# Second mixture of an attention + two-mixture kernel: results kept in PSUM until their split, preparation issued by elapsed products, a second combining buffer, copies of partial sums issued first

## The chip, the cores and the metric

The kernel runs on one core of a Trainium2 chip. The metric is the device time of one execution in microseconds (us), median over runs. TensorE (PE) multiplies, VectorE (DVE), ScalarE (ACT) and GpSimd (POOL) do the elementwise work, SyncE (SP) issues the DMAs. Each engine works through its own list of instructions in order, and semaphores tie the lists together.

## The reference

Clustered attention (queries see only keys of their own cluster), then two feed-forward "mixtures". The change lies in the second:

```python
def _moe2_ref(x, w_gate, w_val, w_out):      # x 1536 x 512, d_ff = 1536
    g = x @ w_gate
    silu = g * (1.0 / (1.0 + np.exp(-g)))
    val = x @ w_val
    return (silu * val @ w_out).astype(np.float32)
```

## The kernel before

Attention fills the first part of the execution, the first mixture the time up to about 517 us, the second mixture the rest. All products are made of fp32r halves: an operand is split into a rounded high part (ACT copies it, "hi") and the remainder (DVE or POOL subtract, "lo"), and a product takes three matmuls (high*high, high*low, low*high).

The weights come in as doubles, in blocks of 128 x 512. A block is loaded into one of two `raw` buffers (line 78), its bits are put together to fp32 by ACT (`block_shift`, line 82) and DVE (lines 91 and 95) in a buffer `cw`, and then split.

**Sets.** The second mixture has 12 blocks f of 128 hidden columns, taken in pairs, and two halves u of the tokens (2 x 384 each): 24 sets `(f, u)` in the order (2k,0) (2k+1,0) (2k,1) (2k+1,1). Weights of f are used by two sets, two places apart. Sets 0 to 3 are plain (`run_plain`): for each e of the two token quarters a gate product g and a value product v (12 matmuls each, a bank of PSUM each), then `v_plain` (ACT sigmoid, DVE sigmoid*g) and `v_plain2` (DVE times v, ACT hi, DVE lo). Sets 4 to 23 use Winograd's form of Strassen's scheme (`run_set`): seven products P1, P2, P6, P7, P5, P3, P4 of 6 matmuls (x 384 columns) instead of eight, in three banks A, B and C (`BANK`, line 946). Bank A runs on: P1 is summed into it, a copy p1 of the partial sum is taken by ACT (`snap`, line 971), P6 is added, copy u2, P5 is added, copy u4, P3 is added. So P6 can't start before copy p1 is done, P5 not before u2, P3 not before u4. The gates and values are then put together by DVE and ACT:

- `v_ga`: p1 + B is the gate of quarter 0; `v_sa`: its sigmoid (ACT); `v_gs`: their product.
- `v_vb`: u4 + C; `v_sb`: sigmoid of A (the gate of quarter 1); `v_b`: A*sigmoid, times u4.
- `v_a`: u2 + C, times the gate product. `hi2`/`lo2` split the two results into g.

Between the products stand six `piece`s per set: 3 matmuls x 512 columns each, which multiply the g of earlier sets by w_out into four banks of their own (`ps_a`); after each second f their sums are moved on (`evac2`, lines 1032 to 1042: DVE adds, or ACT copies and POOL adds). A, B, C of a set, and g0, v0, g1, v1 of a plain set, come from a ring of four banks, `ps_h`: a product waits until the bank's last reader of four allocations ago is done.

**Preparation.** The scheme needs sums of the weights S1 to S4 (POOL, `w_sum`, line 785) and, per half u, sums of the inputs T1 to T4 (DVE, `y_sum`, line 767), each split as well (hi: lines 799 and 759; lo: lines 803 and 763). These steps are `tasks` with an engine and a list of steps that must have been issued before. `hook(engine, n)` (line 1054) stands at fixed places of the sets and issues the first n tasks of that engine whose needs were issued; `finish` forces tasks that a set is about to use. Whether a task's data is there yet doesn't count in the choice.

Of the kernel before, what the change touches and what calls it, by code (L numbers as in the profile page):

```python
# [20 lines left out]
def tile_kernel(ctx, tc, q_t, k_t, q_s, k_s, v_l, cent, w_in, w_out, a_co, b_co, w_gate, w_val, w_o2, out):  # L21
# [4 lines left out]
    P = 128  # L26
# [589 lines left out]
    with ExitStack() as mctx:  # L616
# [126 lines left out]
        cq = cw[:, 0:4 * DM].rearrange("p (i n) -> p i n", i=8)  # L743
# [41 lines left out]
        def w_sum(q):  # L785
# [12 lines left out]
        def w_hi(f, to, frm):  # L798
            nc.scalar.copy(out=w_of(f)[:, 0, to], in_=cq[:, frm])

        def w_lo(f, to, frm):
            w = w_of(f)
# [6 lines left out]
        def c_of(n):  # L809
            key, f, _ = loads[n]  # L810
            i = n % 5 if n < N1 else {"v": 0, "g": 1, "p": 4}[key]
            return cw[:, i * DM:(i + 1) * DM]
# [134 lines left out]
        live2 = {}  # L947

        def short(name):
            return ring(tmp, "short", 10, C3)  # L950

        def pe(s, p):
# [6 lines left out]
            n, last = 0, 6 * (len(terms) // 2) - 1  # L959
            for a, b in zip(terms[::2], terms[1::2]):  # L960
# [20 lines left out]

        def v_ga(s):
            dve(s, "p1", "p1", "B", ALU.add)

        def v_sa(s):
            sigmoid(s, "sa", "p1")

        def v_gs(s):
            dve(s, "p1", "p1", "sa", ALU.mult)
# [7 lines left out]
        def v_b(s):  # L997
            dve(s, "sb", "A", "sb", ALU.mult)
            dve(s, "u4", "u4", "sb", ALU.mult)

        def v_a(s):
            dve(s, "u2", "u2", "C", ALU.add)
            dve(s, "u2", "u2", "p1", ALU.mult)

        def hi2(s, e):
            f, u = sets[s]
            g = g_hl[2 * u + e, f] = g_tile(6, C3)
            nc.scalar.copy(out=g[:, 0, :], in_=live2[s, "u4" if e else "u2"])

        def lo2(s, e):  # L1010
            f, u = sets[s]
            g = g_hl[2 * u + e, f]
            nc.vector.tensor_tensor(  # L1013
                out=g[:, 1, :], in0=live2[s, "u4" if e else "u2"], in1=r32(g[:, 0, :]), op=ALU.subtract
            )
# [3 lines left out]
        def piece(f, j, c, bank=None):  # L1019
# [3 lines left out]
            g, w = g_hl[j, f], wt_of["p", f]  # L1023
            for m, (wi, gi) in enumerate(((0, 0), (1, 0), (0, 1))):
# [7 lines left out]
        def evac2(f, j, c, on_dve):  # L1032
# [5 lines left out]
            else:  # L1038
                ts = tmp[:, 10 * C3:10 * C3 + T]
# [8 lines left out]
        done = set()  # L1048
        asked = set()

        def task(name, engine, needs, fn):
            tasks[name] = (engine, needs, fn)

        def hook(engine, n=1):
            for name in list(tasks):
                eng, needs, fn = tasks[name]
                if n and eng == engine and done.issuperset(needs):
                    del tasks[name]
                    fn()
                    done.add(name)  # L1060
                    n -= 1

        def finish(names):
            for name in names:
                if name in tasks:
                    eng, needs, fn = tasks.pop(name)
                    finish(needs)
                    fn()
                    done.add(name)

        def begin(n):
            while len(started) < min(n, len(loads)):
                block_start()

        def to_prepare(f):
# [15 lines left out]
            for q, needs in ((S1, [(f, "v", "bits")]), (S3, [(f, "v", "bits"), (f, "g", "bits")]), (S2, [(f, S1), (f, S3)]),  # L1091
                             (S4, [(f, S2)])):
                task((f, q), "pool", needs, lambda q=q: w_sum(q))
            A, Sq = slice(0, 3), slice(3, 7)
            task((f, "hi a"), "act", [(f, "g", "bits")], lambda: w_hi(f, A, slice(1, 4)))
# [4 lines left out]
            task((f, "hi p"), "act", [(f, "p", "bits")], lambda: block_hi(started[b + 2], p_place(f)))  # L1100
# [18 lines left out]
        done.update((0, q, "lo") for q in (B11, B12, B21, B22))  # L1119

        def v_plain(s, e):

            name = "u4" if e else "u2"
            live2[s, name] = short(name)
            nc.scalar.activation(out=live2[s, name], in_=live2[s, f"g{e}"], func=AF.Sigmoid)
            dve(s, name, name, f"g{e}", ALU.mult)

        def v_plain2(s, e):
            name = "u4" if e else "u2"
            dve(s, name, name, f"v{e}", ALU.mult)  # L1130
            hi2(s, e)
            lo2(s, e)

# [8 lines left out]
        to_combine(0, [], (T4, T2))  # L1142
        pe(0, "g0")
        hook("dve", 2)
# [4 lines left out]
        hook("dve", 2)  # L1149
        pe(0, "v0")  # L1150
        v_plain2(0, 0)
        mm, ev = project(*seq[NS - 1])
        for fn in mm:
            fn()
        for e in ev:
            e()
        to_combine(1, [B11, B21, B12, B22], (B21, B22, T4, T2))
        hook("act", 2)
        pe(0, "g1")
        hook("dve")  # L1160
        v_plain(0, 1)
        hook("dve")
        hook("pool")
        pe(0, "v1")
        hook("act", 2)
        v_plain2(0, 1)
        hook("dve", 2)
        hook("pool")
# [9 lines left out]
        def run_plain(s, fill):  # L1178
            fill = list(fill)
            n = (len(fill) + 2) // 3  # L1180
            for e in range(2):
                pe(s, f"g{e}")
                hook("act")
                hook("dve")
                hook("pool")
                v_plain(s, e)
                hook("act")
                hook("dve")
                some(fill, n)
                pe(s, f"v{e}")  # L1190
                hook("act")
                hook("dve")
                hook("pool")
                some(fill, len(fill) if e else n // 2)
                v_plain2(s, e)
                hook("dve")

        def run_set(s, fill):
            fill = list(fill)
            f, u = sets[s]  # L1200
# [5 lines left out]
            hook("dve")  # L1206
            pe(s, "P2")
            hook("act")
# [111 lines left out]
```

## Time and profile before

| | |
|---|---|
| three runs, median (range) | 839.53 us (835.87 to 840.25) |
| profiled execution: time / span | 839.48 / 837.7 us |
| busy PE / DVE / ACT / POOL | 94% / 76% / 61% / 56% |
| granted clock, mean | 0.986 |
| second mixture, sets 4 to 23 | 564.80 to 824.43 us |

PE is busy 94% of the span, so the question in any stretch is what PE waits for there and at which clock it runs. Between 300 and 507 us PE has no gap. In the second mixture it has many short ones, each ended by the copy of a partial sum, and a few ended by POOL or DVE. Other engines' idle time only matters where it ends such a gap.

### The profile page before, as it was taken

Reading aid. Unit: us, or ns where it says so; the run is one execution under the profiler, and the core shown is the slowest. Engines: PE = TensorE matmul, PEld = TensorE weight load, DVE = VectorE, ACT = ScalarE, POOL = GpSimd, SP = SyncE. Lnnn points to the kernel's source line nnn. Section 1 sums busy time; section 2 is a strip of 40 time slices with the busy share of each in tenths; the row PEclk is TensorE's granted clock in tenths of the full one; section 3 lists DMA queues with packets and bytes.
Section 4 is the critical chain, followed back from the end, with each engine's and each line's share of the span. In section 5 each row is a group of like instructions: output and inputs, shape, how many; then the busy total and the mean of one; then the engine's idle time right before and its main releaser. Section 6 shows DMA issues by size and latency. Waiting matters only on the chain.

```text
span 837.7 us, 11534 instructions
## 1 busy us (share of the span) xinstructions
PE 791.4 (94%) x4080; PEld 638.0 (76%) x4080; DVE 635.3 (76%) x923; ACT 512.0 (61%) x982; POOL 466.9 (56%) x379
## 2 busy tenths in 40 slices
PE   5999999999999999999999999888997999899997
PEld 4666666666658788888888888877886888888896
DVE  6877788778669999889888898844686766756654
ACT  5767676777776878787687775444534454444431
POOL 3656687557335776767776967643354554444511
PEclk8999999999999999999999999988999999999999
DMA  5256435542222212121112010021211112121013
GB/s 172 92 192 201 146 103 174 194 139 68 70 95 75 76 51 76 50 67 42 69 51 76 27 50 26 1 75 56 97 51 56 70 51 76 50 76 51 1 38 113
DMA packets 26553, 67.94 MB, mean 81 GB/s; under 512 B 4448, under 2 KB 9536, under 8 KB 26496
## 3 DMA queue, kind: packets, MB, share of 16 engines
q1 hardware_dynamic: 26496, 67.21, 24.2%
q8 instruction: 32, 0.52, 0.3%
q14 instruction: 25, 0.20, 0.1%
HBM read 59.48 MB, written 3.19 MB: 75 GB/s over the span
## 4 chain that ended last, share of the span: by engine, by line
PE 57%; DVE 19%; ACT 9%; issue 6%; DMA 5%; POOL 4%; ACTq 0%; DVEq 0%; SPq 0%; POOLq 0%
PE h_ps L664 11%; PE acc L720 10%; PE c_ps L965 9%; PE acc L1025 7%; PE o_ps L437 7%; PE t_ps L426 5%; DVE tmp L976 5%; PE s_ps L368 4%; DMA raw<-w_o_dram 3%; PE s_ps L372 3%; DVE g L1013 2%; DVE st L380 2%; DVE part L1037 1%; DMA raw<-w_out_dram 1%; POOL tmp L681 1%
## 5 line engine op out<-in xcount | busy, mean ns | idle before, releaser
L965 PE MATMUL c_ps<-r,wb 128*128 128x384 f32 x648 | 128.7, 340 | 13.4 <-ACT tmp L973 9.8
L965 PEld LDWEIGHTS c_ps<-r,wb 128*128 128x128 f32 x648 | 115.1, 189 | 23.6 <-ACT tmp L973 13.8
L380 DVE TENSOR_REDUCE st<-s_ps 128x1 f32<-128x768 f32 x96 | 91.4, 952 | 31.7 <-PE s_ps L372 31.2
L388 ACT ACTIVATE p<-s_ps,st 128x768 f32<-128x768 f32 x96 | 87.6, 913 | 19.9 <-DVE st L380 18.3
L431 ACT COPY pt<-t_ps 128x384 f32<-128x384 f32 x160 | 70.2, 485 | 36.1 <-PE t_ps L426 36.0
L681 POOL TENSOR_TENSOR tmp<-tmp 128x512 f32<-128x512 f32 x46 | 65.8, 1431 | 46.1 <-ACT tmp L680 45.7
L82 ACT ACTIVATE raw<-raw 128x512 f32<-128x512 f32 x68 | 45.8, 675 | 60.4 <-DMA raw<-w_o_dram 33.8
L426 PE MATMUL t_ps<-ident,p 128*128 128x128 f32 x576 | 79.8, 274 | 1.0 <-ACT pt L431 0.8
L965 PE MATMUL c_ps<-r,xw 128*128 128x384 f32 x336 | 68.2, 345 | 10.4 <-ACT tmp L973 8.3
L976 DVE TENSOR_TENSOR tmp<-tmp,c_ps 128x384 f32<-128x384 f32 x76 | 41.6, 547 | 44.5 <-ACT tmp L973 39.5
L791 POOL TENSOR_TENSOR cw<-cw 128x256 f32<-128x256 f32 x40 | 33.1, 832 | 75.3 <-DVE cw L95 74.6
L965 PEld LDWEIGHTS c_ps<-r,xw 128*128 128x128 f32 x336 | 60.8, 192 | 16.2 <-ACT tmp L973 10.4
L704 POOL TENSOR_TENSOR g<-td,tmp 128x512 fp32r<-128x512 f32 x46 | 61.0, 1326 | 20.9 <-DVE td L699 20.9
L437 PE MATMUL o_ps<-pt,v 128*64 128x384 f32 x384 | 72.3, 498 | 0.0
L426 PEld LDWEIGHTS t_ps<-ident,p 128*128 128x128 f32 x576 | 67.3, 141 | 6.3 <-ACT p L388 1.1
L720 PE MATMUL acc<-g,r 128*128 128x512 f32 x288 | 71.1, 396 | 0.3 <-ACT part L727 0.3
L1025 PE MATMUL acc<-wb,g 128*128 128x512 f32 x216 | 62.3, 410 | 2.6 <-ACT part L1035 2.6
L720 PEld LDWEIGHTS acc<-g,r 128*128 128x128 f32 x288 | 53.9, 188 | 13.8 <-ACT part L727 0.8
L664 PE MATMUL h_ps<-r 128*128 128x512 f32 x252 | 61.5, 393 | 0.0
L368 PE MATMUL s_ps<-k,q 128*128 128x512 f32 x192 | 58.7, 387 | 2.4 <-ACT p L388 2.2
L1041 POOL TENSOR_TENSOR part<-tmp,part 128x512 f32<-128x512 f32 x19 | 24.7, 1299 | 60.3 <-ACT tmp L1040 60.3
L664 PEld LDWEIGHTS h_ps<-r 128*128 128x128 f32 x252 | 47.1, 188 | 12.3 <-issue 1.8
(155 smaller groups left out, 1788.5 us busy)
## 6 DMA issues: line engine op xcount, KB each, us to landing
raw<-w_in_dram SPq DMA_DIRECT2D x16, 512.0 KB
raw<-w_out_dram SPq DMA_DIRECT2D x16, 512.0 KB
raw<-w_val_dram SPq DMA_DIRECT2D x12, 512.0 KB
raw<-w_gate_dram SPq DMA_DIRECT2D x12, 512.0 KB
raw<-w_o_dram SPq DMA_DIRECT2D x12, 512.0 KB
xa<-q_t_dram SPq DMA_DIRECT2D x14, 384.0 KB
xa<-k_t_dram SPq DMA_DIRECT2D x14, 384.0 KB
sq<-q_s_dram SPq DMA_DIRECT2D x8, 384.0 KB
```

The source lines that it names most:

```text
L368: nc.tensor.matmul(s_ps[:, lo:hi], t["q1"][:, qs], t["k1"][:, lo:hi], start=True, stop=False)
L380: nc.vector.tensor_reduce(out=st[:, 0, k:k + 1], in_=live["s", b, hp, half, i, e], axis=AX.X, op=ALU.max, negate=True)
L388: nc.scalar.activation(out=p, in_=live.pop(("s", b, hp, half, i, e)), func=AF.Exp, bias=st[:, 0, k:k + 1], accum_out=st[:, 1, k:k + 1],)
L426: nc.tensor.transpose(t_ps[:, j, :], p[:, kb * P:(kb + 1) * P], ident)
L431: nc.scalar.copy(out=pt[:, ks, qc], in_=t_ps)
L437: nc.tensor.matmul(live["o", b, hp, half][e * D:(e + 1) * D, :], heads[b, 2 * hp + e]["v"][:, kb, :], live["pt", b, hp, half, e][:, kb, :] ...
L664: nc.tensor.matmul(h_ps, w[:, wi, cs], x[:, xi, cc, :], start=(n == 0), stop=(n == 3 * NCC - 1))
L681: spread.tensor_tensor(out=tq, in0=tq, in1=tr, op=ALU.add)
L720: nc.tensor.matmul(acc[c], w[:, wi, cs], g[:, gi, :], start=(first and m == 0), stop=(last and m == 2))
L965: nc.tensor.matmul(live2[key], set_of[f][:, wi, a, cs], x[xi][:, kc, :], start=(first and n == 0), stop=(n == last), skip_group_check=True,)
L976: eng.tensor_tensor(out=live2[s, out], in0=live2[s, a], in1=live2[s, b], op=op)
L1025: nc.tensor.matmul(acc2[j, c], g[:, gi, c * P:(c + 1) * P], w[:, wi, :], start=(f % 2 == 0 and m == 0), stop=(f % 2 == 1 and m == 2),)
```

## The change

PE and the DMAs keep their order; the lists of ACT, DVE and POOL are reordered.

- Sums and products are written back to their PSUM bank: `v_ga` and `v_gs` write to B, `v_b` to A, `v_a`'s product to B, the plain sets' product to v's bank, and hi2/lo2 read them there. Bank C comes from `ps_a` instead of `ps_h`.
- In `run_set` a snap stands directly behind its product, ahead of piece, sigmoid and hook.
- Odd f above 1 gather their weights in a second buffer `cqs[1]` in `tmp`, so only f-2's splits must be done before f's bits, not f-1's. The ring of short buffers shrinks from 10 to 5 for that.
- `clk` counts products issued (1 for 6 matmuls of 384 columns, 0.65 for a piece). A task is taken only if each need comes from its own engine or was issued at least LAG units ago (ACT, DVE 1.7; POOL 3.5; DMA 5.5). Splits also wait for the set from which their place is free.
- Hooks stand at more places, also ahead of set 1, and weights of f = 2 and 3 are asked for earlier.

```diff
-        cq = cw[:, 0:4 * DM].rearrange("p (i n) -> p i n", i=8)
+        cqs = [
+            t.rearrange("p (i n) -> p i n", i=8) for t in (cw[:, 0:4 * DM], tmp[:, 5 * C3 + T:5 * C3 + T + 4 * DM])
+        ]
...
         def short(name):
-            return ring(tmp, "short", 10, C3)
+            return ring(tmp, "short", 5, C3)
...
-                live2[key] = ps_h.tile([P, T], F32, tag="h", name="c_ps")[:, 0:C3]
+                bank = ps_a.tile([P, T], F32, tag="acc", name="c_ps") if key[1] == "C" else ps_h.tile(
+                    [P, T], F32, tag="h", name="c_ps")
+                live2[key] = bank[:, 0:C3]
...
         def v_ga(s):
-            dve(s, "p1", "p1", "B", ALU.add)
+            dve(s, "B", "p1", "B", ALU.add)
...
         def v_gs(s):
-            dve(s, "p1", "p1", "sa", ALU.mult)
+            dve(s, "B", "sa", "B", ALU.mult)
...
         def v_b(s):
-            dve(s, "sb", "A", "sb", ALU.mult)
-            dve(s, "u4", "u4", "sb", ALU.mult)
+            dve(s, "A", "sb", "A", ALU.mult)
+            dve(s, "A", "u4", "A", ALU.mult)
...
         def v_a(s):
             dve(s, "u2", "u2", "C", ALU.add)
-            dve(s, "u2", "u2", "p1", ALU.mult)
+            dve(s, "B", "u2", "B", ALU.mult)
...
+        LAG = {"act": 1.7, "dve": 1.7, "pool": 3.5, "dma": 5.5, "set": 0.0}
+        def in_time(eng, by, at):
+            return by == eng or at + LAG[by] <= clk[0]
...
-                if n and eng == engine and done.issuperset(needs):
+                if n and eng == engine and all(x in done and in_time(eng, *done[x]) for x in needs):
...
-                before = [x for x in [(loads[n - 2][1], loads[n - 2][0], "bits")] if x[0] > 1]
-                task((f, key, "shift"), "act", before, lambda n=n: block_shift(started[n]))
-                old = [(f - 1, x) for x in ("lo a", "lo s", S1, S2, S3, S4, "lo p") if f > 2 and (x == "lo p") == (key == "p")]
+                task((f, key, "shift"), "act", [("load", n)], lambda n=n: block_shift(started[n]))
+                old = [(f - 1, "lo p")] if key == "p" else [(f - 2, "lo a"), (f - 2, "lo s")]
+                old = [x for x in old if x[0] > 1]
...
         def run_set(s, fill):
             pe(s, "P1")
+            snap(s, "p1")
             some(fill)
-            snap(s, "p1")
...
             pe(s, "P6")
+            snap(s, "u2")
+            v_sa(s)
             some(fill)
-            v_sa(s)
-            snap(s, "u2")
             hook("dve")
             v_gs(s)
+            hook("act")
             pe(s, "P7")
-            hook("act")
...
             pe(s, "P5")
             snap(s, "u4")
+            hook("act")
+            hook("dve")
             v_vb(s)
...
             pe(s, "P4")
+            hi2(s, 1)
+            v_a(s)
+            lo2(s, 1)
             some(fill)
-            v_a(s)
-            hi2(s, 1)
-            lo2(s, 1)
...
             if s >= PLAIN:
-                finish([(f, x) for x in ("hi a", "lo a", "hi s", "lo s")])
+                finish([(f, x) for x in ("hi a", "lo a")])
```

ACT's list in set 15, before, from hi2 at the end of set 14 on: L973 is a snap (p1, u2, u4 in turn), L1008 hi2, L980 a sigmoid, L82 a weight shift, L1040 the copy of `evac2`.

```order
L1008 CAST g<-tmp 128x384
L973 COPY tmp<-c_ps 128x384
L1008 CAST g<-tmp 128x384
L980 ACTIVATE tmp<-tmp 128x384
L973 COPY tmp<-c_ps 128x384
L82 ACTIVATE raw<-raw 128x512
L973 COPY tmp<-c_ps 128x384
L1040 COPY tmp<-acc 128x512
L980 ACTIVATE tmp<-c_ps 128x384
L799 CAST wb<-cw 128x768
```

The same of the changed kernel (the lines are those of the changed file: L983 a snap, L1021 hi2, L990 a sigmoid, L803 and L103 weight splits, L1052 the copy of `evac2`).

```order
L1021 CAST g<-c_ps 128x384
L983 COPY tmp<-c_ps 128x384
L1021 CAST g<-c_ps 128x384
L983 COPY tmp<-c_ps 128x384
L990 ACTIVATE tmp<-c_ps 128x384
L803 CAST wb<-tmp 128x768
L983 COPY tmp<-c_ps 128x384
L103 CAST wb<-cw 128x512
L990 ACTIVATE tmp<-c_ps 128x384
L1052 COPY tmp<-acc 128x512
```

The second snap (u2) now stands ahead of the sigmoid, and no shift stands between the second and the third: a weight split stands there instead, and shifts stand at other places.

DVE's list before, from the lo2 of set 1's first quarter (not shown) to the multiplication by g0 of set 2 (the last row, which releases that bank for set 3): L767 sums T, L976 multiplications, L1013 lo2, L763 lo of an input sum.

```order
L767 TENSOR_TENSOR part<-part 128x2x384
L976 TENSOR_TENSOR tmp<-tmp,c_ps 128x384
L767 TENSOR_TENSOR part<-part 128x2x384 x2
L976 TENSOR_TENSOR tmp<-tmp,c_ps 128x384
L1013 TENSOR_TENSOR g<-tmp,g 128x384
L763 TENSOR_TENSOR r_67<-part,r_67 128x768 x2
L976 TENSOR_TENSOR tmp<-tmp,c_ps 128x384
```

The same stretch after (L769 sums T, L986 multiplications, L1026 lo2, L765 lo, L91 and L95 the bits of weights); the last row is again the multiplication by g0 of set 2.

```order
L91 TENSOR_SCALAR cw<-raw 128x512
L769 TENSOR_TENSOR part<-part 128x2x384
L986 TENSOR_TENSOR tmp<-tmp,c_ps 128x384
L769 TENSOR_TENSOR part<-part 128x2x384
L765 TENSOR_TENSOR r_67<-part,r_67 128x768
L95 SCALAR_TENSOR_TENSOR cw<-raw,cw 128x512
L986 TENSOR_TENSOR c_ps<-tmp,c_ps 128x384
L1026 TENSOR_TENSOR g<-c_ps,g 128x384
L91 TENSOR_SCALAR cw<-raw 128x512
L95 SCALAR_TENSOR_TENSOR cw<-raw,cw 128x512
L986 TENSOR_TENSOR tmp<-tmp,c_ps 128x384
```

Four instructions for weights (L91, L95) now stand ahead of that multiplication, and lo2 reads the PSUM bank of v, which so stays in use until lo2 is done.

## Rows read from the trace of the kernel before

**Rows 1.** Windows by set: stretch, length, busy time (instructions) per engine, PEclk, DMA.
```profile
507.73:564.80 57.07, 51.66 (x253) 47.11 (x252) 42.12 (x51) 27.11 (x46) 33.91 (x20) 0.94 0.09 28
564.80:582.21 17.41, 14.46 (x62) 13.02 (x61) 5.14 (x10) 6.35 (x13) 4.58 (x5) 0.80 0.17 62
...
632.71:649.42 16.71, 12.24 (x61) 10.53 (x60) 12.16 (x16) 5.81 (x12) 9.32 (x7) 1.00 0.14 42
...
700.62:713.23 12.61, 11.74 (x62) 10.66 (x61) 8.82 (x14) 6.50 (x13) 7.57 (x6) 1.00 0.20 69
...
790.06:801.60 11.54, 11.54 (x62) 10.73 (x60) 6.25 (x12) 3.79 (x8) 2.87 (x3) 1.00 0.00 1
...
813.04:824.43 11.39, 11.39 (x61) 10.68 (x60) 6.24 (x12) 3.79 (x8) 1.29 (x2) 1.00 0.19 71
824.43:837.70 13.27, 8.32 (x37) 6.57 (x35) 6.88 (x12) 1.61 (x3) 1.78 (x2) 0.91 0.42 158
...
564.80:824.43 259.63, 237.77 (x1201) 215.69 (x1200) 167.44 (x265) 111.60 (x217) 108.35 (x81) 0.99 0.16 55
```

**Rows 2.** Waits of PE, 564.8 to 824.43: total us, times, longest.
```profile
PE c_ps L965 <- ACT tmp L973: 18.1, 16, 2.9
PE c_ps L965 <- POOL xw L803: 2.1, 1, 2.1
```

**Rows 3.** Timeline of PE: start, us, engine, line, operation, count [idle before <-releaser].
```profile
544.00 3.25 PE L965 MATMUL c_ps<-r,wb 128*128 128x384 f32 x12 [1.93 <-DVE tmp L976]
...
557.55 3.14 PE L1025 MATMUL acc<-wb,g 128*128 128x512 f32 x9 [2.62 <-ACT part L1035]
...
702.38 2.25 PE L965 MATMUL c_ps<-r,wb 128*128 128x384 f32 x12
704.46 0.85 PE L1025 MATMUL acc<-xw,g 128*128 128x512 f32 x3
705.15 1.21 PE L965 MATMUL c_ps<-r,wb 128*128 128x384 f32 x6
707.23 1.32 PE L965 MATMUL c_ps<-r,wb 128*128 128x384 f32 x6 [0.87 <-ACT tmp L973]
...
722.50 1.31 PE L965 MATMUL c_ps<-r,wb 128*128 128x384 f32 x6 [1.16 <-ACT tmp L973]
```

**Rows 4.** Timeline of ACT in sets 14 and 15.
```profile
706.29 0.52 ACT L980 ACTIVATE tmp<-tmp 128x384 f32<-128x384 f32 x1 [1.84 <-DVE tmp L976]
706.72 0.46 ACT L973 COPY tmp<-c_ps 128x384 f32<-128x384 f32 x1
...
721.43 0.65 ACT L82 ACTIVATE raw<-raw 128x512 f32<-128x512 f32 x1 [3.46 <-DMA raw<-w_o_dram]
721.98 0.46 ACT L973 COPY tmp<-c_ps 128x384 f32<-128x384 f32 x1
```

**Rows 5.** DVE groups by form, 564 to 824.5: busy us, mean ns | idle before.
```profile
L1013 DVE TENSOR_TENSOR g<-tmp,g 128x384 fp32r<-128x384 f32 x39 | 38.6, 989 | 1.9 <-ACT g L1008 1.9
L976 DVE TENSOR_TENSOR tmp<-tmp 128x384 f32<-128x384 f32 x58 | 38.4, 662 | 6.0 <-ACT tmp L980 4.3
L976 DVE TENSOR_TENSOR tmp<-tmp,c_ps 128x384 f32<-128x384 f32 x60 | 32.8, 547 | 42.4 <-ACT tmp L973 39.5 <-PE c_ps L965 2.7
...
L91 DVE TENSOR_SCALAR cw<-raw 128x512 uint32<-128x512 uint32 x27 | 17.9, 661 | 0.0
```

**Rows 6.** Timeline of DVE, plain sets and set 15.
```profile
501.08 0.76 DVE L684 SCALAR_TENSOR_TENSOR h_ps<-tmp,cst,h_ps 128x512 f32<-128x512 f32 x1
...
536.55 1.95 DVE L767 TENSOR_TENSOR part<-part 128x768 f32<-128x768 f32 x2 [1.28 <-POOL r L763]
...
539.54 0.56 DVE L1013 TENSOR_TENSOR g<-tmp,g 128x384 fp32r<-128x384 f32 x1 [0.58 <-ACT g L1008]
...
543.40 0.54 DVE L976 TENSOR_TENSOR tmp<-tmp,c_ps 128x384 f32<-128x384 f32 x1
...
717.43 0.68 DVE L95 SCALAR_TENSOR_TENSOR cw<-raw,cw 128x512 uint32<-128x512 uint32 x1
```

More of the change, by code (lines that the diff above doesn't have):

```diff
@@ L783, in p_home, with w_sum @@
             return r[:, at:at + BLK]
-        def w_sum(q):
+        def w_sum(f, q):
+            cq = cqs[f % 2 if f > 1 else 0]
             a, b, op = {
@@ L1007, in hi2 @@
             g = g_hl[2 * u + e, f] = g_tile(6, C3)
-            nc.scalar.copy(out=g[:, 0, :], in_=live2[s, "u4" if e else "u2"])
+            nc.scalar.copy(out=g[:, 0, :], in_=live2[s, "g", e])
         def lo2(s, e):
@@ L1065, in finish @@
                 if name in tasks:
[L1066 to L1069, printed above, removed]
+                    finish(tasks[name][1])
+                    run(name)
         def begin(n):
             while len(started) < min(n, len(loads)):
+                done["load", len(started)] = "dma", clk[0]
                 block_start()
@@ L1092, in to_prepare @@
                              (S4, [(f, S2)])):
-                task((f, q), "pool", needs, lambda q=q: w_sum(q))
+                task((f, q), "pool", needs, lambda q=q: w_sum(f, q))
             A, Sq = slice(0, 3), slice(3, 7)
-            task((f, "hi a"), "act", [(f, "g", "bits")], lambda: w_hi(f, A, slice(1, 4)))
+            room = ("set", 2 * f - 4 if f % 2 == 0 else 2 * f - 3)
+            task((f, "hi a"), "act", [(f, "g", "bits"), room], lambda: w_hi(f, A, slice(1, 4)))
             task((f, "lo a"), "pool", [(f, "hi a")], lambda: w_lo(f, A, slice(1, 4)))
@@ L1098, in to_prepare @@
             task((f, "lo s"), "pool", [(f, "hi s")], lambda: w_lo(f, Sq, slice(4, 8)))
-            task((f, "hi p"), "act", [(f, "p", "bits")], lambda: block_hi(started[b + 2], p_place(f)))
+            room = ("set", f // 2 * 4 - 2)
+            task((f, "hi p"), "act", [(f, "p", "bits"), room], lambda: block_hi(started[b + 2], p_place(f)))
             task((f, "lo p"), "pool", [(f, "hi p")], lambda: block_lo(started[b + 2], wt_of["p", f]))
@@ L1118, in tile_kernel, with hooks @@
         begin(N1 + 8)
-        done.update((0, q, "lo") for q in (B11, B12, B21, B22))
+        done.update({(0, q, "lo"): ("pool", -9.0) for q in (B11, B12, B21, B22)})
         def v_plain(s, e):
[L1123 to L1126, printed above, removed]
+            live2[s, "sa"] = short("sa")
+            nc.scalar.activation(out=live2[s, "sa"], in_=live2[s, f"g{e}"], func=AF.Sigmoid)
+            live2[s, f"u{e}"] = live2[s, "sa"]
+            dve(s, f"u{e}", "sa", f"g{e}", ALU.mult)
         def v_plain2(s, e):
-            name = "u4" if e else "u2"
-            dve(s, name, name, f"v{e}", ALU.mult)
+            dve(s, f"v{e}", f"u{e}", f"v{e}", ALU.mult)
+            live2[s, "g", e] = live2[s, f"v{e}"]
             hi2(s, e)
             lo2(s, e)
+        def hooks(n=1):
+            for eng in ("act", "dve", "pool"):
+                hook(eng, n)
         _, reciprocal, quotient, remainder = pipe.pop()
@@ L1142, in tile_kernel @@
         to_combine(0, [], (T4, T2))
+        to_prepare(2)
+        clk[0] += 2
         pe(0, "g0")
-        hook("dve", 2)
+        hooks()
         mm, _ = project(*seq[NS - 2])
@@ L1148, in tile_kernel @@
         v_plain(0, 0)
-        hook("dve", 2)
+        hooks()
+        clk[0] += 1.4
+        hooks()
+        clk[0] += 1.4
         pe(0, "v0")
+        hooks()
         v_plain2(0, 0)
@@ L1154, in tile_kernel @@
             fn()
+        hooks()
+        clk[0] += 2.7
         for e in ev:
@@ L1157, in tile_kernel @@
         to_combine(1, [B11, B21, B12, B22], (B21, B22, T4, T2))
+        for key in [x for x in tasks if x[0] == 2 and len(x) < 4 and x[0] != 1]:
+            tasks[key] = tasks.pop(key)
         hook("act", 2)
         pe(0, "g1")
-        hook("dve")
+        hooks()
         v_plain(0, 1)
-        hook("dve")
-        hook("pool")
+        hooks()
         pe(0, "v1")
-        hook("act", 2)
+        hooks()
         v_plain2(0, 1)
-        hook("dve", 2)
-        hook("pool")
+        hooks()
         def some(fill, n=1):
@@ L1251, in tile_kernel @@
             f, u = sets[s]
-            if s % 2 == 0 or s == 1:
-                to_prepare(s // 2 + 2)
+            done["set", s] = "set", clk[0]
+            for x in ((2,), (2, 3))[s > 1] if s < 4 else (s // 4 * 2 + 2, s // 4 * 2 + 3):
+                to_prepare(x)
             if s == 2:
```

69 lines of the change are left out of this document (38 added, 31 removed).

## The prediction

> **What bounds the kernel now.** I read three views in this order: busy time and granted clock by set, then PE's waits, then the timelines of PE and ACT around two of those waits.
>
> By sets [rows 1], PE's busy time per set changes little (11.39 to 12.24 us; 14.46 in set 4, at a clock of 0.80), but the sets last 11.4 to 17.4 us. The last sets, for which no weights are prepared any more, take 11.54 and 11.39 us with PE busy throughout at clock 1.00. That is the floor for 7 products and 6 pieces. The twenty sets 4 to 23 take 259.63 us. At the mean of the two floors, 11.47, they would take 229.4: 30.2 us are lost there, in gaps, refills behind them, and that low clock.
>
> The gaps have one main cause [rows 2]: 18.1 us in 16 waits of PE for ACT's copy of a partial sum (L973), and 2.1 for one late weight split on POOL. The timelines show why the copy is late. In set 14 P2 and P6 start at 702.38, the piece at 704.46, P7 at 705.15, so 6 matmuls take 1.04 us and a piece 0.69 [rows 3]. P6 ended near 704.46, but ACT made copy u2 only at 706.72, behind a sigmoid that had itself waited 1.84 us for DVE [rows 4]; P5 then started at 707.23 instead of 706.2. In set 15 the third copy stood behind a weight shift that waited 3.46 us for its DMA, and P3 waited 1.16 [rows 3, 4]. ACT is not short of time (6.50 us busy in a set of 12.61 [rows 1]); it is held up by what stands first in its list.
>
> **The change part by part.**
>
> *Copies first.* A copy now stands directly behind its product in ACT's list. It takes 0.46 us [rows 4] and PE needs it only 1.04 + 0.69 = 1.73 us after the product (P1 to P6, P6 to P5) or two pieces, 1.38, after P5. What stands ahead of it in ACT's list must be over by the product's end: hi2, one hook task and the earlier sigmoid, each with at least one product's time for it. So a copy has about 0.9 to 1.2 us of slack, and all 18.1 us of waits should go, with the refill behind each. If the cover is gone (a shift that waits more than a microsecond for its DMA right ahead of a copy), a wait of today's size, 0.9 to 1.2, comes back at that place.
>
> *Order by elapsed products, second combining buffer.* A shift is issued 5.5 units behind its load, some 5.7 us at 1.04 per product. The load of set 15 landed 721.43 - 718.11 = 3.3 us after the bits that freed its buffer (717.43 + 0.68) [rows 4, 6]. DVE may so run 2.4 us late before a shift waits. Through the second buffer and the earlier requests, the split of the sums for f = 5, which ended the 16.71 us of set 9, is issued in set 8 before P5, five products and five pieces ahead of P6 of set 9 (5 x 1.04 + 5 x 0.69 = 8.7 us); I cost it at nothing and count the 2.1 as gone. What is late next: nothing in PE's list that I can find.
>
> *Results in PSUM.* Seven products and sums and two lo2 per set stay as many instructions. Products of two SBUF buffers take 662 ns in the mean, those with a bank as an operand 547 [rows 5]; writing a bank costs nothing visible (0.76 for 512 columns, 501.08 [rows 6]). lo2 takes 989 in the mean today against 0.56 where POOL is idle [rows 5, 6], so DVE's work can shrink by up to 3 x 0.115 + 2 x 0.43 = 1.2 us per set. That is off PE's path: 0 in the sum. At worst DVE stays at today's 8.8 us in a set of 11.5. Bank C moves to the ring of the pieces: four allocations per set from four banks, so each comes back to its own use a set later, long after its last reader. A and B are held until lo2, but the ring is four deep and a set takes two, so they are next written two sets on. Both 0.
>
> *The plain sets.* Here I expect a loss. Set 3's g0 must wait until DVE has multiplied by set 2's g0, today at 543.40 + 0.54 = 543.94, and PE, ready at 542.07, waits 1.93 [rows 3, 6]. In the new list the same sums and remainders stand ahead of that, so I correct today's end: minus the 1.28 that DVE waited for POOL's split, which is now issued a product earlier; plus four weight instructions, 2 x 0.66 + 2 x 0.68 = 2.68 [rows 5, 6]; plus the hold of one bank until lo2, 0.58 + 0.56 = 1.14 [rows 6]. That gives 546.5, 2.5 us later than now; PE's waits up to there are then 1.93 + 2.5 = 4.4, spread over sets 1 and 2, where four banks come round, so about 1.1 at each. From there to set 4 the kernel now takes 564.80 - 544.00 = 20.8, with a wait of 2.62 for ACT's evacuation behind a DMA [rows 3], which the lag rule removes, and a clock of 0.94 over the 57.07 us, which is 0.06 x 57.07 = 3.4 us of products lost at half clock [rows 1]. Without both, set 4 would start at 546.5 + 20.8 - 2.6 - 3.4 = 561.3, 3.5 earlier than now.
>
> Does the clock fall again? Today it did behind waits of 1.93, 2.62 and more (12 products took 3.25 instead of 2.25 at 544.00) and didn't behind 0.87 and 1.16 [rows 3]. The new waits lie near the lower pair, but close together. I grant half of the 3.4: set 4 starts at 563.0, 1.8 earlier. Bounds: no waits at all gives 564.80 - 5.4 (57.07 - 51.66 idle) - 3.4 = 556.0; the waits above with today's clock give 564.7, and with as much clock lost again 568.
>
> The Trainium skill (TensorE: Matmul & The Clock Gate, Part 1) says that the array's clock is gated to half when the engine has idled and comes back once it has been busy. The trace agrees in kind, 0.80 in the set with the longest gaps against 1.00 in the others [rows 1]; by the rule the new waits may cost as much clock as today's, and the time would be 809.2 instead of 807.5.
>
> *Sum.* The profiled execution took 839.48, 1.78 more than its span, and its time is within 0.1 of the median 839.53. Start of set 4: -1.8. Twenty sets at the floor: -30.2. The tail behind 824.43 (13.27 [rows 1]) is the last pieces and the output, unchanged: 0. Span 837.7 - 32.0 = 805.7, time 807.5.
>
> **The rivals.**
>
> *Half of the waits stay.* Each pair of sets still prepares a weight block with three shifts on ACT, and a shift is late as soon as DVE runs over 2.4 us behind, which it does in the plain sets and where POOL holds it up (lo2 at 989). With one wait of 0.75 per set the twenty sets lose 15: 837.7 - 1.8 - 15.2 = 820.7, time 822.5. For it: 3.46 at a single DMA [rows 4]. Against it: the copies of one set then stand ahead of the shifts of the next hook.
>
> *It does not do what it says.* The copies come first but wait for something else that I don't see, and the sets keep their length: only the plain part moves, 837.7 ± 3, time about 838. Against it: every late copy I looked at stood behind another instruction, with its product long done.
>
> *DVE becomes the bound (slower).* PE's banks now come free by lo2 and DVE's multiplications alone. In set 9 DVE was busy 12.16 us [rows 1]. If the added bank traffic makes that the rule, with two waits of 0.58 for hi2 per set [rows 6], a set takes 13.3 and A and B are released late: 20 x 13.3 = 266, 6.4 more than now, and with set 4 starting 3 late, time 849. It decides only from 13 us of DVE work per set. Against it: DVE's busy time is 8.8 in a usual set [rows 1], and the operations lose their second SBUF operand.
>
> **How the numbers follow.** Forecast 0.71, half of the waits 0.18, no effect 0.05, slower 0.06. A measurement of this kernel can tell 0.5%, 4.2 us, from no change. Faster takes the forecast and half of the waits: 0.89; same 0.05; slower 0.06. The forecast's own range is 800.5 (set 4 at 556.0) to about 814 (set 4 at 568 and 0.1 lost per set). To hold 8 in 10, the range reaches on to the rival of half the waits: 801 to 822.
>
> **What would show it.** Right: sets 6 to 20 of 11.4 to 11.6 us each, PE's waits for the partial-sum copy below 3 us in total, clock 1.00 from set 5 on, set 9 no longer than its neighbours; in sets 1 to 3 waits of PE for lo2 and for the multiplications, 4 to 6 us in total. Wrong: waits for the copy (or for ACT behind a weight load) of over 0.3 per set, or DVE busy above 10 us per set.

## The result and the profile after

The changed kernel took 809.41 us in the median of four runs (807.8 to 812.15), against 839.17 us (835.87 to 840.25) for the kernel before on the same chip: a ratio of 0.9655, with a 95% interval of 0.9616 to 0.9695. The profiled execution has a span of 808.6 us, 29.1 less than before.

By sets (windows: stretch, length, busy time and instructions of PE, PEld, DVE, ACT and POOL, granted clock, DMA share, GB/s), the stretches that answer to [rows 1] are the plain sets, set 4, set 5, sets 10 and 16, the tail, and the twenty sets in one:

```profile
506.64:561.85 55.21, 50.47 (x254) 45.76 (x253) 47.17 (x52) 26.61 (x44) 33.89 (x21) 0.97 0.11 39
561.85:576.98 15.13, 13.33 (x62) 12.05 (x60) 7.87 (x14) 9.75 (x19) 8.87 (x7) 0.89 0.32 106
576.98:588.57 11.59, 11.59 (x61) 10.79 (x60) 8.45 (x14) 6.80 (x13) 4.03 (x4) 1.00 0.27 90
634.24:645.82 11.58, 11.58 (x62) 10.77 (x60) 7.59 (x14) 6.41 (x13) 7.50 (x6) 1.00 0.15 47
703.40:714.80 11.40, 11.40 (x61) 10.68 (x60) 7.57 (x14) 5.85 (x12) 6.76 (x5) 1.00 0.08 20
561.85:795.30 233.45, 231.65 (x1202) 215.78 (x1201) 151.50 (x266) 113.29 (x220) 98.02 (x80) 0.99 0.18 59
```

From set 5 on PE is busy from end to end at clock 1.00: the nineteen sets last 233.45 - 15.13 = 218.32 us, 11.49 each. Set 4 alone is 3.6 us over that. The twenty sets lost 26.2 us of their 259.63, the plain sets 1.86 of their 57.07. The second mixture also began 1.1 us earlier, in work that the change doesn't touch, and the tail stayed (13.30 for 13.27): together the 29.1. That 1.1 is no more than chance: over the profiled executions of all kernels here the second mixture begins between 504.1 and 510.0 us. So differences of 2 or 3 us between two times below say little by themselves; the windows from there on say more.

PE's waits from 500 us on (total, times, longest), against [rows 2] and [rows 3]:

```profile
PE c_ps L975 <- DVE g L1026: 4.4, 3, 2.1
PE c_ps L975 <- ACT tmp L983: 1.8, 1, 1.8
PE acc L720 <- POOL g L704: 0.3, 1, 0.3
```

The first line is the plain sets, the second is set 4, the third still belongs to the first mixture. Sixteen waits for a copy have become one. PE's timeline in set 15, where [rows 3] had a gap before P3 of the set, now reads without one:

```profile
696.49 2.25 PE L975 MATMUL c_ps<-r,wb 128*128 128x384 f32 x12
698.57 0.84 PE L1037 MATMUL acc<-xw,g 128*128 128x512 f32 x3
699.26 0.85 PE L1037 MATMUL acc<-tdw,g 128*128 128x512 f32 x3
699.94 1.21 PE L975 MATMUL c_ps<-r,wb 128*128 128x384 f32 x6
```

ACT's timeline beside it, to be read against [rows 4]. A copy now waits for PE and nothing else, and what was ahead of it stands behind it:

```profile
696.00 0.48 ACT L983 COPY tmp<-c_ps 128x384 f32<-128x384 f32 x1 [1.85 <-PE c_ps L975]
696.38 0.50 ACT L990 ACTIVATE tmp<-c_ps 128x384 f32<-128x384 f32 x1
696.76 0.84 ACT L803 CAST wb<-tmp 128x768 fp32r<-128x768 f32 x1
698.77 0.48 ACT L983 COPY tmp<-c_ps 128x384 f32<-128x384 f32 x1 [1.17 <-PE c_ps L975]
```

DVE's groups by form from 561.85 to 795.30, against [rows 5]: the subtraction of the lower half fell from 989 to 552 ns, the products from 662 to 561.

```profile
L986 DVE TENSOR_TENSOR c_ps<-tmp,c_ps 128x384 f32<-128x384 f32 x100 | 56.1, 561 | 43.0 <-ACT tmp L990 39.5 <-PE c_ps L975 2.1
L1026 DVE TENSOR_TENSOR g<-c_ps,g 128x384 fp32r<-128x384 f32 x39 | 21.5, 552 | 4.0 <-ACT g L1021 4.0
```

### The profile page after: what moved, and what is told of

It reads as the page before. It is cut to its first block, busy times and chain, and to the rows that moved or that the text cites. A ratio compares the mean times of both kernels' runs of the same rounds, so it can differ in the third digit from the quotient of the medians.

```text
span 808.6 us, 11528 instructions
## 1 busy us (share of the span) xinstructions
PE 782.2 (97%) x4080; PEld 635.6 (79%) x4080; DVE 626.6 (77%) x923; ACT 512.5 (63%) x982; POOL 455.4 (56%) x379
## 4 chain that ended last, share of the span: by engine, by line
PE 69%; DVE 16%; ACT 6%; POOL 3%; issue 3%; DMA 2%; DVEq 0%; ACTq 0%; POOLq 0%; SPq 0%
PE c_ps L975 18%; PE acc L1037 11%; PE h_ps L664 10%; PE acc L720 9%; PE o_ps L437 7%; PE t_ps L426 5%; PE s_ps L368 4%; PE s_ps L372 3%; DVE st L380 2%; DVE td L696 1%; ACT p L388 1%; DVE sm L327 1%; POOL tmp L681 1%; DVE td L699 1%; DVE g L693 1%
## 5 line engine op out<-in xcount | busy, mean ns | idle before, releaser
L975 PE MATMUL c_ps<-r,wb 128*128 128x384 f32 x648 | 126.5, 338 | 0.3 <-DVE g L1026 0.2
L986 DVE TENSOR_TENSOR c_ps<-tmp,c_ps 128x384 f32<-128x384 f32 x108 | 60.5, 560 | 43.1 <-ACT tmp L990 39.5
L983 ACT COPY tmp<-c_ps 128x384 f32<-128x384 f32 x60 | 28.9, 481 | 78.2 <-PE c_ps L975 78.2
L975 PE MATMUL c_ps<-r,xw 128*128 128x384 f32 x336 | 66.4, 341 | 1.8 <-ACT tmp L983 1.8
L82 ACT ACTIVATE raw<-raw 128x512 f32<-128x512 f32 x68 | 45.7, 678 | 28.0 <-DMA raw<-w_in_dram 12.1
L1037 PE MATMUL acc<-wb,g 128*128 128x512 f32 x216 | 60.1, 398 | 0.0
L368 PEld LDWEIGHTS s_ps<-k,q 128*128 128x128 f32 x192 | 28.7, 189 | 35.8 <-ACT pt L431 15.6
```

Source lines behind the costliest of these rows:

```text
L368: nc.tensor.matmul(s_ps[:, lo:hi], t["q1"][:, qs], t["k1"][:, lo:hi], start=True, stop=False)
L975: nc.tensor.matmul(live2[key], set_of[f][:, wi, a, cs], x[xi][:, kc, :], start=(first and n == 0), stop=(n == last), skip_group_check=True,)
L1037: nc.tensor.matmul(acc2[j, c], g[:, gi, c * P:(c + 1) * P], w[:, wi, :], start=(f % 2 == 0 and m == 0), stop=(f % 2 == 1 and m == 2),)
```

## The experiments

All times are medians. The kernel before took 839.1 to 840.0 us in the runs beside them, and 837.9 beside the one with the load's lag only and two of the last three.

### Is it the place of the copies?

*Before, with copies first:* each copy directly behind its product, and the ACT hook between P7 and P5 ahead of P7.

```diff
+            snap(s, "u2")
             some(fill)
             v_sa(s)
-            snap(s, "u2")
...
             v_gs(s)
+            hook("act")
             pe(s, "P7")
-            hook("act")
```

> The kernel before with nothing changed but the place of the copies in ACT's list: each copy of a partial sum directly behind its product, and the ACT task that stood between P7 and P5 moved ahead of P7. Theory (the place of the copies in ACT's list cost most): the 18.1 us of waits for copies and the refills behind them mostly go, the waits for late weight splits (3.8 us) and the plain sets stay: 815 to 822 us. Rival 1 (the preparation's order, with shifts that wait for their DMA, cost most): ACT is still stopped by shifts ahead of copies, 828 to 836 us.

Measured: 832.41 us (ratio 0.9915, 0.9884 to 0.9945), a quarter of the way. My theory fell short here, and rival 1 holds. PE's waits for copies went from 18.1 us in 16 to 13.3 in 9, and one wait for an evacuation in the plain sets grew from 2.6 to 4.2:

```profile
PE c_ps L965 <- ACT tmp L973: 13.3, 9, 2.6
PE acc L1025 <- ACT part L1035: 4.2, 1, 4.2
```

ACT's timeline shows what the copies still stand behind:

```profile
644.21 0.65 ACT L82 ACTIVATE raw<-raw 128x512 f32<-128x512 f32 x1 [3.91 <-DMA raw<-w_o_dram]
644.76 0.46 ACT L973 COPY tmp<-c_ps 128x384 f32<-128x384 f32 x1
...
668.67 0.65 ACT L82 ACTIVATE raw<-raw 128x512 f32<-128x512 f32 x1 [3.22 <-DMA raw<-w_o_dram]
669.23 0.46 ACT L973 COPY tmp<-c_ps 128x384 f32<-128x384 f32 x1
```

The copy has nothing to wait for, but a shift that waits for its load is ahead of it, and PE starts the next product at 645.27 after a wait of 2.62 us, and at 669.74 after 1.10. With this the sixteen waits of before fall into two kinds, of which [rows 3] has one each: seven behind such a shift (1.16 at 722.50; 10.6 us together; in six the copy is the next instruction, in set 4 a sigmoid stands between) and nine elsewhere (0.87 at 707.23, behind a sigmoid; 7.5 together). Copies first leaves the seven, now 11.2 us, and two others of 2.1 together.

*The changed kernel with the copies at their old places*, the same edit in reverse:

```diff
-            snap(s, "u2")
             v_sa(s)
+            snap(s, "u2")
...
             v_gs(s)
-            hook("act")
             pe(s, "P7")
+            hook("act")
```

> The changed kernel with the copies back at their old places in ACT's list (behind piece and sigmoid, the ACT hook between P7 and P5 again), all else as changed. Theory: a wait of about 0.9 us for copy u2 or u4 comes back in most of the twenty sets, 820 to 830 us. Rival 1 (the preparation's order is what counted): no shift waits long any more, so copies are in time wherever they stand, 809 to 814 us.

Measured: 814.76 us (0.9679), 5.4 more than the change and just above the rival's range; five waits of PE for copies, 4.3 us together. Four of them are 1.0 us each and the theory's own mechanism, though in four sets and not in most: the copy stands behind a sigmoid that waits 3.1 us for DVE.

```profile
652.47 0.49 ACT L990 ACTIVATE tmp<-c_ps 128x384 f32<-128x384 f32 x1 [3.11 <-DVE c_ps L986]
652.85 0.47 ACT L983 COPY tmp<-c_ps 128x384 f32<-128x384 f32 x1
```

Both ways the place of the copies is worth 5 to 7 us, not the 18.1 and more of the forecast's step.

### Is it the lag behind a load?

*Before, with copies first and the lag:* a shift is issued only 5.5 products after its load.

```diff
+                early = name[-1] == "shift" and clk[0] < issued.get(name, 1e9) + 5.5
-                if n and eng == engine and done.issuperset(needs):
+                if n and eng == engine and done.issuperset(needs) and not early:
...
```

> The kernel before with early copies as in the first experiment (832.4 us, PE's waits for ACT's copies 13.3 us in 9), and besides a shift on ACT is issued no earlier than 5.5 products after its load was issued. Results in SBUF, one combining buffer. Theory A (what was left of the copies' waits is ACT held in front of a copy by a shift that waits for its DMA: 4.83, 3.91, 3.22, 3.33, 3.26 us before the copies that came 1.1 to 2.6 us late): ACT's DMA waits fall from 38 to under 8 us and PE's waits for copies from 13.3 to under 4; without another cost 818 to 822 us. Theory B (the same, but one buffer makes the splits of each odd f late, forced at the set's head): the copies' waits go, and PE waits for POOL 2 to 4 us in up to five sets: 825 to 838 us. Rival C (the copies' waits hang on DVE and the slots of the ring, not on the shift): copies' waits stay at 10 us or more, time within 2 us of 832.

Measured: 823.76 us (0.982, 0.9786 to 0.9853). PE's waits in this kernel:

```profile
PE c_ps L967 <- POOL wb L803: 7.8, 4, 2.4
PE c_ps L967 <- POOL xw L803: 4.8, 2, 2.4
PE c_ps L967 <- DVE tmp L978: 2.5, 2, 1.9
PE acc L720 <- POOL g L704: 0.3, 1, 0.3
```

No wait for a copy is left; so the held shifts were all that remained of them. But the steps behind a later shift are later too, and with one combining buffer the splits of f = 3, 5, ... come too late: 12.6 us for POOL. Theory B's mechanism, at a price just below its range.

*The changed kernel without that lag* (the constant for loads 0, those between engines kept):

```diff
-        LAG = {"act": 1.7, "dve": 1.7, "pool": 3.5, "dma": 5.5, "set": 0.0}
+        LAG = {"act": 1.7, "dve": 1.7, "pool": 3.5, "dma": 0.0, "set": 0.0}
```

> The changed kernel with the lag after a load's issue at 0 in place of 5.5 products; the lags of 1.7 and 3.5 between engines stay. Theory A (this lag is what frees ACT's list): shifts hold ACT 2 to 4 us for their DMA again, 8 times or more, PE waits 1 to 2 us for a copy about once per part f: 815 to 824 us. Rival (early copies and results in PSUM leave enough slack that a held ACT costs nothing; the lags between engines matter): ACT's DMA waits return but PE's do not, 808 to 812 us.

Measured: 826.12 us (0.9859), 16.7 more than the change: theory A's mechanism, at a price above its range. ACT's groups show the shifts held 46.6 us by their loads (5.2 in the changed kernel), and PE waits 9.6 us in five for copies, up to 2.4. Its plain sets are longer as well, 61.1 us from the first product to set 4 for 55.2. The shifts' group:

```profile
L82 ACT ACTIVATE raw<-raw 128x512 f32<-128x512 f32 x30 | 20.1, 671 | 46.6 <-DMA raw<-w_o_dram 27.2 <-DMA raw<-w_val_dram 17.9 <-DMA raw<-w_gate_dram 1.6
```

*With that lag only*, and the split of the four sums held until its region is free:

```diff
-        LAG = {"act": 1.7, "dve": 1.7, "pool": 3.5, "dma": 5.5, "set": 0.0}
+        LAG = {"act": 0.0, "dve": 0.0, "pool": 0.0, "dma": 5.5, "set": 0.0}
...
-            task((f, "hi s"), "act", [(f, S4)], ...
+            task((f, "hi s"), "act", [(f, S4), room], ...
```

> The changed kernel with only the lag after a load's issue (5.5 products) kept; the lags between engines (1.7 for ACT and DVE, 3.5 for POOL) at 0, and the split of the four sums of f held until the set in which its region is free. Theory A (the load's lag alone frees ACT's list; a step that waits for DVE or POOL holds an engine too briefly to matter): ACT's DMA waits stay at 4 to 8 us, PE's waits for copies under 3 us, 808 to 813 us. Rival (the lags between engines matter as well: ACT or DVE stands in front of a copy or a product's sum for 1 to 3 us while POOL finishes sums or splits of 2 us each): PE's waits rise by 5 us or more, 815 to 826 us.

Measured: 810.40 us (0.9668), the time of the change. ACT's shifts wait 0.0 us for loads, and from 562 to 800 us PE is busy for all of the 238 us:

```profile
L82 ACT ACTIVATE raw<-raw 128x512 f32<-128x512 f32 x30 | 20.4, 679 | 0.0
```

```profile
562.00:800.00 238.00, 238.00 (x1240) 221.47 (x1240) 152.55 (x271) 113.62 (x222) 98.48 (x79) 1.00 0.18 60
```

Theory A holds: of the four lags one does the work.

*With no lag at all:* in this kernel part of the second mixture is computed from other weights, since in the change only the lag keeps the split of f's four sums behind the last use of S4 of f - 3 in the same region.

```diff
-            return by == eng or at + LAG[by] <= clk[0]
+            return True
```

> The changed kernel with the lag of every need set to nothing, so tasks are issued as soon as their needs were issued, as before the change. Theory: some shifts wait for their DMA again, but most behind the copies; 809 to 816 us. Rival 1: shifts stop ACT ahead of copies again, 820 us and more.

Measured: 832.75 us (0.9895). Its PE waits 7.2 us in four for just that split on POOL, which the change doesn't have, so its 23 us are no measure of the lags; the two runs above are.

### Is it the second combining buffer?

*The changed kernel with one buffer*, and the order that one buffer needs:

```diff
-            ... for t in (cw[:, 0:4 * DM], tmp[:, 5 * C3 + T:5 * C3 + T + 4 * DM])
+            ... for t in (cw[:, 0:4 * DM], cw[:, 0:4 * DM])
...
-                old = ... else [(f - 2, "lo a"), (f - 2, "lo s")]
+                old = ... else [(f - 1, "lo a"), (f - 1, "lo s")]
```

> The changed kernel with one combining buffer for all parts f, as before the change; order by elapsed products, PSUM results and early copies stay. With one buffer the bits of f may be written only after the splits of f-1, and with the lags kept the splits of every odd f (3, 5, 7, 9, 11) are then issued by force at the head of the set that needs them. Theory A (the forecast's term for the second buffer: only the one wait of 2.1 us for POOL, 1 time in the kernel before): 810 to 813 us, one POOL wait. Theory B (the lag is only affordable with the second buffer, because it stretches a part's preparation beyond one part's time): PE waits for POOL in five sets, 2 to 4 us each with the refills, 10 to 20 us in all: 820 to 832 us.

Measured: 836.64 us (0.9969, 0.994 to 0.9998). That is 27.2 more than the change and more than theory B allowed: without the second buffer nearly all of the gain is gone. PE waits 17.6 us in nine for POOL, in five sets. The timeline of PE and the windows of sets 12 to 14 show why they cost more than their length:

```profile
678.92 1.65 PE L975 MATMUL c_ps<-r,wb 128*128 128x384 f32 x4 [2.45 <-POOL wb L807]
680.37 1.48 PE L1037 MATMUL acc<-wb,g 128*128 128x512 f32 x3
...
685.50 1.47 PE L975 MATMUL c_ps<-r,wb 128*128 128x384 f32 x4 [1.81 <-POOL wb L807]
686.77 1.48 PE L1037 MATMUL acc<-wb,g 128*128 128x512 f32 x3
```

```profile
664.37:675.95 11.58, 11.58 (x61) 10.72 (x60) 7.98 (x16) 4.77 (x11) 2.03 (x3) 1.00 0.29 92
675.95:695.56 19.61, 15.35 (x62) 13.36 (x61) 9.74 (x16) 6.58 (x13) 9.52 (x8) 0.83 0.13 40
695.56:707.01 11.45, 11.45 (x62) 10.70 (x61) 8.08 (x16) 6.05 (x12) 4.15 (x6) 1.00 0.34 117
```

The set in the middle holds two waits, of 2.45 and 1.81 us, 4.26 together, and is 8.1 us longer than its neighbours: the rest is products at a lower clock (a piece of three matmuls takes 1.48 us in place of 0.85). It is the costliest of the five; the others are 2.6 to 6.0 us longer than the usual 11.5.

### Are the results in PSUM free?

*The changed kernel with all results in SBUF*, two buffers and five slots for short results:

```diff
-            dve(s, "B", "p1", "B", ALU.add)
+            dve(s, "p1", "p1", "B", ALU.add)
...
-            dve(s, "B", "u2", "B", ALU.mult)
+            dve(s, "u2", "u2", "p1", ALU.mult)
...
```

> The changed kernel with sums and products in SBUF again (as in the kernel before), in the plain sets too; banks, order and lags as changed. Theory (PSUM as the place of results is worth nothing by itself off PE's path, and costs in the plain sets, where it holds banks until lo2): sets 5 to 23 stay at 11.4 to 11.6 us, PE's waits in the plain sets fall from 4.4 to under 2 us: 804 to 809 us. Rival 2 (results in PSUM keep DVE clear of POOL, without which DVE is late): DVE busy per set rises by over 1 us and waits for copies or banks come back, 813 to 825 us.

Measured: 818.68 us (0.973), 9.3 more than the change, in rival 2's range. In the profiled executions the difference is 8.7, of which 2.3 lie before the second mixture, 1.1 in the plain sets and 5.4 behind them. PE waits 7.6 us in four for copies, one in set 4 and three of 1.9. DVE's timeline in one of those sets, then ACT's:

```profile
637.03 2.22 DVE L1026 TENSOR_TENSOR g<-tmp,g 128x384 fp32r<-128x384 f32 x1
639.17 0.68 DVE L1049 TENSOR_TENSOR part<-acc,part 128x512 f32<-128x512 f32 x1
639.77 2.17 DVE L91 TENSOR_SCALAR tmp<-raw 128x512 uint32<-128x512 uint32 x1
641.98 0.69 DVE L95 SCALAR_TENSOR_TENSOR tmp<-raw,tmp 128x512 uint32<-128x512 uint32 x1
642.59 0.55 DVE L1026 TENSOR_TENSOR g<-tmp,g 128x384 fp32r<-128x384 f32 x1
```

```profile
643.23 0.48 ACT L983 COPY tmp<-c_ps 128x384 f32<-128x384 f32 x1 [4.07 <-DVE g L1026]
```

The copy waits for DVE because its slot still holds the last set's result, until the subtraction at 642.59 has read it; and that is late because operations of 0.55 us take 2.2 beside a split on POOL.

*The same with that subtraction ahead of DVE's prepared steps*, which was meant to take away the slot wait and leave the longer operations:

```diff
                 hi2(s - 1, 0)
+                lo2(s - 1, 0)
             hook("dve", 2)
             pe(s, "P2")
-            if s > PLAIN:
-                lo2(s - 1, 0)
```

> The kernel with all results in SBUF (818.7 us; PE waits 7.6 us in 4 for ACT's copies, of which 1.82 in set 4 for the held shift) with one edit: the lower half of the first result of a set, which frees the ring's slot that the next set's second copy needs, is issued right behind its upper half and so ahead of two prepared steps on DVE. Theory A (what SBUF results cost in the formula sets is the slot: the result occupies it until a subtraction that stands behind steps of 2.2 us on DVE, and the copy waits for that 4.0 us, three times): the three waits of 1.9 us go, 809 to 813 us. Rival (the cost is DVE's longer operations with two SBUF sources beside POOL, 770 and 927 ns in place of 561 and 552, wherever the step stands): the waits come up at another place, 816 to 820 us.

Measured: 815.92 us (0.9717, 0.9686 to 0.9748), between the two theories. The three waits shrank from 1.9 to 0.8 or 0.9 and a fourth of 0.65 came. But the slot wait wasn't taken away, only shortened, from 4.07 to 3.00 us:

```profile
644.75 0.48 ACT L983 COPY tmp<-c_ps 128x384 f32<-128x384 f32 x1 [3.00 <-DVE g L1026]
```

```profile
642.37 2.30 DVE L1026 TENSOR_TENSOR g<-tmp,g 128x384 fp32r<-128x384 f32 x1
```

The subtraction stands earlier, but takes 2.30 us beside POOL's split in place of 0.55. So the slot and DVE's length act in one chain: the copy waits for the slot, and the slot for a slow operation. This run can't price them apart, and a ring of ten slots beside two buffers, which would have told, wasn't tried. In the change the second buffer lies where half of the ring was, so the results in PSUM are also what makes room for it.

### What is left

In the changed kernel's set 4 the wait of 1.80 us before P6 goes back to the one mechanism again, a shift held by its load at the end of set 3 (ACT's timeline, cut):

```profile
561.46 0.68 ACT L82 ACTIVATE raw<-raw 128x512 f32<-128x512 f32 x1 [2.60 <-DMA raw<-w_o_dram]
562.04 0.47 ACT L1146 ACTIVATE tmp<-c_ps 128x384 f32<-128x384 f32 x1
...
566.06 0.48 ACT L983 COPY tmp<-c_ps 128x384 f32<-128x384 f32 x1
```

Three kernels went for this and for the plain sets. The first edit is in all three: the shift of part 3's w_o is issued a set later. The second kernel also writes the plain sets' second product into SBUF; the third instead puts DVE's prepared steps in the plain sets behind the multiplication.

```diff
-                task((f, key, "shift"), "act", [("load", n)], ...
+                task((f, key, "shift"), "act", [("load", n)] + [("set", 4)] * (n == N1 + 11), ...
```

```diff
-            dve(s, f"v{e}", f"u{e}", f"v{e}", ALU.mult)
+            dve(s, f"u{e}", f"u{e}", f"v{e}", ALU.mult)
```

```diff
                 pe(s, f"v{e}")
-                hooks()
+                hook("act")
+                hook("pool")
...
                 v_plain2(s, e)
+                hook("dve")
                 hooks()
```

> The changed kernel with one edit: the shift of part 3's w_o is issued a set later (the plain sets as changed). Theory A (of the 2.7 us that this edit won together with the edit on the plain sets, all came from set 4, whose 15.13 us fell to 11.52; the other edit only moved the plain sets' waits): 805 to 807.5 us, PE's waits 4.4 us in three, no wait from set 4 on. Rival (the plain sets' edit had a part in it): 808 to 810 us.

> The changed kernel with two edits at what PE still waits for: in the plain sets the second product's result goes to SBUF instead of into v's own PSUM bank (so the bank is free at the multiplication and not after the second half's subtraction on DVE), and the shift of part 3's w_o, which held ACT 2.6 us for its DMA at 561, is issued a set later. Theory A (each removes its wait: plain sets 4.4 us to about 1, set 4's 1.8 to 0, and the low clock that follows them, 0.7 us a time for two or three windows): 801 to 805 us. Rival (the waits move: the plain sets wait for ACT or for DVE's queue instead, the shifted load comes late in set 5 or 6): 807 to 812 us.

> As the kernel with the later shift, and besides DVE's prepared steps in the plain sets stand behind the second product's multiplication and subtraction and no longer in front of them. Theory A (DVE reaches a multiplication late because two splits of 2.6 us each, lengthened by POOL's split beside them, stand ahead of it; the waits are 2.09 and 2.10 us and each is followed by a lower clock): both waits under 0.5 us, plain sets 55.2 to 51 or 52, 801 to 804 us. Rival (DVE is simply full in the plain sets, 48.6 of 55.4 us, so the same waits come up one product later): 805 to 808 us.

Measured: 807.36, 806.76 and 806.15 us (ratios 0.9627, 0.9624 and 0.9621, each within 0.004). The first edit removes set 4's wait in all three; in the first kernel the set is at the floor:

```profile
562.75:574.30 11.55, 11.55 (x62) 10.74 (x61) 5.25 (x10) 7.64 (x15) 5.85 (x5) 1.00 0.28 93
```

The plain sets didn't give: PE waits 5.9, 5.8 and 5.7 us there, not each time at the same products, and from the first product to set 4 they take 55.2, 56.3 and 56.3 us for 55.2 in the changed kernel. From set 4 to the end they take 243.2, 243.1 and 243.1 for 246.8, which is set 4's 3.6. Theory A of the first holds in its time and in set 4; its plain sets have four waits of 5.9 together and not three of 4.4. In the other two the rivals' mechanism does, in the second at a time just under its range. DVE is busy 47 to 49 of these 55 or 56 us, so a wait that is removed comes up one product later. These are the best versions measured, but 2 to 3 us below the changed kernel is less than the runs can tell apart.

## Why the prediction was right, and where its terms were wrong

807.5 was forecast and 809.4 came; the sum held, the attribution didn't.

- *Twenty sets at the floor.* Nineteen are, at 11.49 us for 11.47. Set 4 is not: +3.6. There the rival "half of the waits stay" holds, by its own mechanism, in one set of twenty.
- *The plain sets.* Waits of 4.4 us were worked out and 4.4 came, though as two of 2.1 and one of 0.25 and not four of 1.1. Set 4 was to start 1.8 earlier; the stretch is 1.86 shorter. Half of the clock's loss was granted back; the clock rose from 0.94 to 0.97. That the number fits is in part luck, for the clock's term isn't borne out: in the kernel with only the later shift the plain sets ran at clock 1.00 and took the same 55.2 us, with 5.9 us of waits in place of 4.4. DVE's releases set the time up to the last wait, and a faster clock only waits longer for them. Behind the last wait a low clock does cost: in the one-buffer kernel it came there, and the plain sets took 56.5.

```profile
507.52:562.75 55.23, 48.97 (x253) 44.36 (x252) 48.72 (x55) 28.09 (x47) 34.82 (x23) 1.00 0.12 39
```

- *Copies first: "all 18.1 us of waits should go."* This step failed. Alone it removed the kind that was 7.5 of them. The exception that the step itself named, a shift that waits over a microsecond right ahead of a copy, was no exception: it made seven of the sixteen waits and 10.6 of the 18.1 us, that behind the 3.46 us of [rows 4] among them. Copies first left these; with the lag besides no wait for a copy was left.
- *The second buffer: 2.1 us.* Mis-sized. It was counted only for one wait of the kernel before, but it also pays for the lag: taken away, it costs 27.2.
- *Results in PSUM: 0.* Mis-sized: taken away, they cost 9.3. The step saw DVE's 1.2 us per set as off PE's path, but not the slot that a result holds until a subtraction that POOL can lengthen. DVE's busy time per set fell from 8.4 to 7.6 us (167.44 and 151.50 over twenty).
- *The tail.* 0 forecast, 13.30 for 13.27.
- *The start.* Nothing was forecast; its 1.1 us of the 29.1 are no more than chance.

The sum was right because it was made from PE's gaps in the windows and not from the parts: what fills the gaps was seen, what each part does towards it was not. Taken out one at a time, the parts cost 5.4, 16.7, 27.2 and 9.3 us, 58.6 together, twice the gain of 29.8: the parts aren't independent, and what one is worth hangs on the others.

## What to carry to other kernels

When an instruction is late behind others in its engine's list, look at what the head of the list waits for, and count late instructions by that head, before costing a reordering: moving the late one forward helps only where nothing that waits for a DMA is still ahead. A later issue lengthens the chain behind it, so it has to come with the buffer that lets the chain overlap; cost the two as one term. An edit with no cost on the critical engine can still hold a buffer's slot, and what that costs depends on how late the last reader of the slot can be.

## What the runs showed of the hardware

DVE's operations with two SBUF operands lose more beside POOL than the means of [rows 5] tell: the subtraction at 637.03, shown above, takes 2.22 us with both sources in SBUF beside a split on POOL from 636.66 to 638.84, and 0.55 with one of them in PSUM beside the like split in the changed kernel (the line below from DVE's timeline; POOL's split ran from 634.68 to 636.53). The Trainium skill (GPSIMD Engine Reference, 1. Specifications) says that the two engines share their interfaces to SBUF and that VectorE's instructions with two SBUF inputs contend there; the trace agrees. Two SBUF sources aren't the whole condition: the operation with one source at 639.77, shown above too, took 2.17 us beside POOL's next split (639.25 to 641.67), and 0.41 at 644.59 in the kernel with the subtraction moved ahead, once the split was over.

```profile
634.82 0.55 DVE L1026 TENSOR_TENSOR g<-c_ps,g 128x384 fp32r<-128x384 f32 x1
```

The clock does not follow the length of a wait alone. The same wait of 2.09 us at the same product was followed by six matmuls in 2.07 us in the changed kernel and in 1.32 in the one with the later shift. The changed kernel's next wait of 2.10 us was followed by 1.31, so not each of its two waits has a lower clock behind it, as the last expectation above has it (the first two lines are the changed kernel's PE, the third the other's):

```profile
529.54 2.07 PE L975 MATMUL c_ps<-wb 128*128 128x384 f32 x6 [2.09 <-DVE g L1026]
543.96 1.31 PE L975 MATMUL c_ps<-wb 128*128 128x384 f32 x6 [2.10 <-DVE g L1026]
```

```profile
530.41 1.32 PE L975 MATMUL c_ps<-wb 128*128 128x384 f32 x6 [2.09 <-DVE g L1026]
```

The kernel before shows it too. The prediction read its clock as falling behind waits of 1.93 us and more, but two waits of that size in set 9 were followed by full speed, which the clock of 1.00 in that set [rows 1] had told:

```profile
635.35 0.97 PE L965 MATMUL c_ps<-r,xw 128*128 128x384 f32 x4 [2.12 <-POOL xw L803]
645.86 1.31 PE L965 MATMUL c_ps<-r,xw 128*128 128x384 f32 x6 [1.90 <-ACT tmp L973]
```
